# Spacing the loads of the first two heads and the start of the gate within one stage of a gated attention kernel

## The chip, the cores and the metric

The kernel runs on one core of a Trainium2 chip. The metric is the device time of one execution in microseconds. The kernel before took 2851.99 us (median of three runs, 2851.46 to 2855.48).

## The reference

Two attention blocks read the same input `x` (2048 rows of 1024) and are mixed row by row with a gate. Block A is a linear attention, block B a softmax attention, both with 32 heads of width 32. All tensors are float32. The two blocks are condensed below.

```python
def reference(A_x, A_wqkv, A_wo, B_x, B_wqkv, B_wo, gate_w):
    x = A_x
    g = _sigmoid((x * gate_w).sum(-1, keepdims=True))
    a = _A_ref(x, A_wqkv, A_wo)
    b = _B_ref(x, B_wqkv, B_wo)
    return g * a + (1 - g) * b
...
    # A: phi(t) = (t + 1 or exp(t)) + 1e-6
        kv = jnp.einsum("bhsd,bhse->bhde", phi(k), v)
        o = (phi(q) @ kv) / (phi(q) . sum(phi(k)) + 1e-6)
    # B:
        p = _softmax(q @ k.T * Dh ** -0.5)
        o = p @ v
    # both: o, heads side by side, @ wo
```

## The kernel before

Each float32 operand of a projection is split into a high and a low part, and a product of two such operands takes three matmuls (high by high, high by low, low by high; lines 152, 155 and 157). A first phase computes q and k of block B and the first half of its v, and writes them to DRAM (`qk`, `v`), together with the split rows of x (`xs`). Then a stage that this document calls the stage of v computes the second half of v, one unit for each of the 16 blocks of 128 rows. A unit is 24 matmuls: eight slices `k` of the contraction, three matmuls each. The stage also prepares the first two heads of block B, and computes the gate.

Three buffers hold x for these units, half a unit each: two DMAs of 256 KB (high and low part) fill one. `load_half(m)` issues such a load. It is called after the slices k = 3 and k = 7, for the half three places ahead, whose buffer has just become free.

Into the same units are threaded:

- `first`, a queue of 14 loads for heads 0 and 1. For each head, in this order: the first 512 columns of q (three DMAs of 64 KB, each into 32 partitions), the first 512 columns of k (likewise), the other 1536 columns of q (three DMAs of 192 KB), three further blocks of k (three DMAs of 64 KB each), and v (one DMA of 256 KB in pieces of 128 bytes).
- `gates`, a generator. Its first step loads the gate's weights, broadcast to 128 partitions (512 KB, into `zrep`), and the first block of x by rows (512 KB). Each later step computes one block's dot product on DVE (line 495) and loads the next block; two buffers take turns. Seventeen steps finish it.
- the scores of head 0 for the row maxima: one matmul (line 1123) and one reduction on DVE (line 1128), which frees the score's PSUM bank. 76 of them must be done before the heads' main loop (lines 1297, 1300) begins.
- the store of each unit's v (256 KB), after ScalarE has copied it out of PSUM.

The program is written out in order by a planner at build time. It keeps a clock per engine, with fixed costs for instructions and fixed guesses for when a load will be there, and emits the next item of four streams (`lin` for the units, `max` for the maxima, `head`, `out`) whose start its clock allows. Up to six scores may be emitted ahead of their due time; the others fall due evenly from the sixth unit's end to the fifteenth's. All DMAs of this stage are issued by SP, in the program's order, and every engine runs its own instructions in program order.

After the stage follow the 32 heads, with the linear attention's units between their matmuls, and the output projection.

Of the kernel before, what the change touches and what calls it, by code (L numbers as in the profile page):

```python
# [47 lines left out]
def kernel(  # L48
# [26 lines left out]
    TPC = C // P  # L75
# [63 lines left out]
    def wpart(k, p):  # L139

        o = ((k % 2) * 2 + p) * C
        return w_t[k // 2][:, o:o + C]
# [86 lines left out]
    def ended(items, *also):  # L229

        if any(item.end is None for item in items):
            return None
        return max([0.0, *also] + [item.end for item in items])
# [24 lines left out]
    def take(short=False):  # L258

        idle = ring(short)  # L260
        times = {b: ended(readers[b], free[b]) for b in idle}
        b = min(idle, key=lambda b: (times[b] is None, times[b] or 0.0))
        need(readers[b])
        free[b] = ended(readers[b], free[b])
        readers[b].clear()
        held[b] = True
        return b
# [469 lines left out]
    def pump_w(now=False):  # L737

        while next_w and (now or coming_w and coming_w[0][1] <= T["pe"]):
            follow, k, mark, eng = next_w.popleft()  # L740
            if not coming_w:
                more_w(True)
            split_w(*follow, k, *coming_w.popleft(), eng)
            mark.end = w_ready[k]
            if k + LEAD_W < NK:
                later_w.append((*follow, k + LEAD_W))
            more_w(now)
        more_w(now)
# [88 lines left out]
    def load_mix():  # L837
        assert not mix_here and not stores
        a, c = mix_todo.popleft()
        for i in range(HK):  # L840
            dma(mix_hi[i], a_wo[(a * HK + i) * P:(a * HK + i + 1) * P, c * C:(c + 1) * C])
        mix_here.append((a, c, T["pe"] + 11.0))
# [83 lines left out]
    def linear():  # L926
        extra = iter(())
        gates = gate()
        first = deque()
# [6 lines left out]
        for n, (i, t) in enumerate(units):  # L936
            kind, c = chunks[i]
            follow = chunks[i + 1] if i + 1 < len(chunks) else None
            lag = 2 if kind == "v" else 0

            def renew(k):

                mark = Later(None, 0.0, 0.0, 0, None)
                w_left[k][:] = [mark]
                next_w.append((follow, k, mark, nc.vector if kind == "v" else nc.gpsimd))
                pump_w(kind == "v")

            yield bank_at
            b = take()
            ps = bank[b]  # L950
            T["pe"] = max(T["pe"], free[b])
            lin_kind[0] = kind
            if (kind, c, t) in (("q", 1, 2), ("q", 1, 8), ("o", 0, 2), ("o", 0, 8)):
                load_mix()
            for k in range(NK):
                yield lambda: ended(w_left[k], w_ready[k], xp_ready.get(2 * n + k // HK, 0.0))
                need(w_left[k])
                stat = [xstat_lin(n, k, p) for p in range(2)]
                for m, _ in enumerate(three(ps, stat, (wpart(k, 0), wpart(k, 1)), k)):
                    lin_pe(1.0)  # L960
                    if m < 2:
                        yield always
                store_mix()
                if kind == "v":
                    if k % 2 and first:
                        first.popleft()()
                    if t >= 2 and (k == 2 or k == 6 and t % 2):
                        next(gates, None)
                if k % HK == HK - 1:
                    load_half(2 * n + k // HK + 3)  # L970
                if k == 0 and n + 7 == len(units) and not o_main[0]:
                    load_o(0)
                if k == 1 and n + 1 == len(units):
                    assert finished[0] >= H - 2
                    need(pr_left[extra_pr[2]])
                    xo_t[0] = big_tile(PR[extra_pr[2]], F32R)
                    split_o(0, slice(0, NK - 1))
                if k == NK // 2 and n + 1 == len(units) and over["head"]:
                    split_o(1, slice(0, NK - 1))
                if k == NK - 1:  # L980
                    yield from extra
                if follow and follow[0] == "o":
                    if t == NT - 1:
                        w_left[k].clear()
                        yield lambda: 0.0 if mixed.count((k // HK, follow[1])) == 8 * HK else None
                        load_wa(follow[1], k)
                    continue
                if follow and t == NT - 2 and k == 0:
                    yield lambda: None if mix_here or stores else 0.0
                if follow and t == NT - 2 and k < min(LEAD_W, NK):  # L990
                    coming_w.append(load_w(*follow, k, LEAD_W + 1))
                if follow and t == NT - 1 and k >= lag:
                    renew(k - lag)
            extra = iter(())
            e, r = mid[3 + n % 3], mid[6]
            if kind == "v":
                give(b, use("act", 0.5, T["pe"] + LATENCY["pe"]))
                v_out(c, t, ps, mid[11 - n % 2])
            elif kind == "kv":
                va = mid[7][:, (n % 2) * HC:(n % 2 + 1) * HC]  # L1000
                yield from keys_alone(n - 2)
                nc.scalar.copy(va, ps[:, HC:])
                use("act", 0.28, T["pe"] + LATENCY["pe"])
                end = phi(ps, e, HC)

                def more(end, c=c, t=t, e=e, ps=ps):
                    pk = e[:, :HC]
                    nc.vector.scalar_tensor_tensor(pk, pk, 1.0, ps[:, :HC], op0=ALU.min, op1=ALU.add)
                    z_end[c % 2] = use("pool", 0.69, end)
                    if t == 0:  # L1010
                        nc.gpsimd.tensor_copy(zsum[c % 2], pk)
                    else:
                        nc.gpsimd.tensor_add(zsum[c % 2], zsum[c % 2], pk)

                todo = [defer(more, end, 0.34)]
                give(b, 0.0, todo)
                keys(n, c, t, e, va, todo)
                if t == NT - 1:
                    extra = keysum(c)
            elif kind == "q":  # L1020
                yield lambda: None if n - 3 not in turned and chunks[units[n - 3][0]][0] == "q" else 0.0
                end = phi(ps, e, C)
                d = dn[n % 2]

                def sums(_, e=e, ps=ps):
                    nc.vector.scalar_tensor_tensor(ps, e, 1.0, ps, op0=ALU.min, op1=ALU.add)

                def scaled(_, c=c, ps=ps, r=r):
                    nc.vector.tensor_mul(r, ps, zrep[:, c * C:(c + 1) * C])

                last = []

                def dens(end, r=r, d=d, last=last):
                    nc.vector.tensor_reduce(d, r.rearrange("p (h d) -> p h d", d=DH), AX.X, ALU.add)
                    nc.scalar.add(d, d, eps)
                    last[0].at = use("act", 0.2, end)

                def divide(_, t=t, e=e, ps=ps, d=d):
                    nc.vector.reciprocal(d, d)
                    nc.vector.scalar_tensor_tensor(  # L1040
                        e.rearrange("p (h d) -> p h d", d=DH), ps.rearrange("p (h d) -> p h d", d=DH),
                        g_sb[:, t:t + 1], d.unsqueeze(2).to_broadcast([P, C // DH, DH]),
                        op0=ALU.mult, op1=ALU.mult)

                todo = chain(((sums, 0.63), (scaled, 0.63), (dens, 0.63), (divide, 0.9)), end)
                last.append(todo[-1])
                give(b, 0.0, todo)
                tasks.append((lambda todo=todo: None if kv_todo else both(ended(todo + o_left), o_free[(len(turned) + 1) % 2], bank_at()),
                              lambda n=n, c=c, t=t, e=e, todo=todo: queries(n, c, t, e, todo)))
            else:  # L1050
                res = mid[(7, 10)[n % 2]]
                give(b, use("act", 0.5, T["pe"] + LATENCY["pe"]))
                nc.scalar.copy(res, ps)
                dma(ra_d[t][:, c * C:(c + 1) * C], res)
            if follow and follow[0] != "o" and t == NT - 1:
                for k in range(NK - lag, NK):
                    renew(k)
# [661 lines left out]
```

## Time and profile before

| | |
|---|---|
| median of three runs | 2851.99 us |
| the profiled execution | 2853.72 us |
| its span, first to last instruction | 2852.0 us |
| mean granted clock of TensorE | 0.996 |
| DMA, mean over the span | 150 GB/s |

The page gives each engine's busy time, then the span in 40 slices of 71.3 us, of which each digit is a tenth of the slice. The slices of PE, its granted clock and DMA are the ones to look at here:

```profile
PE   9999998999999999999999999999999999999999
...
PEclk9999998999999999999999999999999999999999
DMA  8867679533344334333434344455656464534642
GB/s 276 248 222 234 208 217 286 169 96 104 96 126 104 102 99 123 96 101 97 132 97 107 97 130 133 147 172 172 195 180 184 132 165 137 157 109 133 198 150 78
```

The seventh slice (428 to 499 us) lies in the stage of v. It is the only one in which PE is under 90% busy and the granted clock under 0.9, and the one with the most DMA traffic.

In the views of single instructions a row gives the start in us from the span's beginning, the duration, the engine, the line, the operation with what it writes and reads, and in brackets how long the engine sat idle before it and what released it. SPq rows are the issuing of DMAs by SP: their duration is the time that SP spent on issuing, not the transfer's.

### The profile page before, as it was taken

The numbers are of one execution on the slowest core, as the hardware profiler recorded it, in microseconds if no ns is written. First come the engines' busy times: TensorE is split into PE (matmuls) and PEld (weight loads), VectorE is DVE, ScalarE is ACT, GpSimd is POOL, SyncE is SP. The second block draws the span as 40 slices with busy tenths as digits, with TensorE's granted clock in tenths as the row PEclk, the third lists the DMA queues.
The fourth block names the chain that finished last, engine by engine and source line by source line (L and its number), as shares of the span: only waits on it lengthen the run. The fifth ranks groups of instructions, "written<-read, shape, count | busy, mean of one in ns | idle before, by whom it ended". The sixth has DMA issues, their size and how long they took to land.

```text
span 2852.0 us, 46554 instructions
## 1 busy us (share of the span) xinstructions
PE 2823.2 (99%) x15944; PEld 2055.9 (72%) x15944; DVE 2232.2 (78%) x3659; ACT 1597.9 (56%) x2994; POOL 1910.0 (67%) x894
## 2 busy tenths in 40 slices
PE   9999998999999999999999999999999999999999
PEld 8888876677767776677667767777776766676787
DVE  7777755788888888888888888788878888887522
ACT  5334320466666666666666666566666666666400
POOL 0000010399999999999999999899889888885000
PEclk9999998999999999999999999999999999999999
DMA  8867679533344334333434344455656464534642
GB/s 276 248 222 234 208 217 286 169 96 104 96 126 104 102 99 123 96 101 97 132 97 107 97 130 133 147 172 172 195 180 184 132 165 137 157 109 133 198 150 78
DMA packets 376714, 428.56 MB, mean 150 GB/s; under 512 B 105007, under 2 KB 210735, under 8 KB 376477
## 3 DMA queue, kind: packets, MB, share of 16 engines
q1 hardware_dynamic: 362876, 412.47, 47.4%
q0 software_dynamic: 13600, 13.11, 3.4%
q8 instruction: 127, 2.08, 0.3%
q14 instruction: 111, 0.90, 0.1%
HBM read 298.06 MB, written 112.98 MB: 144 GB/s over the span
## 4 chain that ended last, share of the span: by engine, by line
PE 96%; DMA 2%; SPq 0%; issue 0%; ACT 0%; DVE 0%; POOL 0%; ACTq 0%
PE bank L1297 17%; PE bank L1123 16%; PE bank L152 15%; PE bank L1454 15%; PE bank L155 15%; PE bank L157 15%; DMA big<-xs 1%; PE bank L1188 1%; PE bank L906 1%; PE bank L795 0%; DMA v<-mid 0%; SPq L169 0%; DMA big<-qk 0%; PE bank L1180 0%; DMA big<-wa 0%
## 5 line engine op out<-in xcount | busy, mean ns | idle before, releaser
L1389 POOL TENSOR_TENSOR big<-big,big 128x512 f32<-128x512 f32 (+2 forms) x694 | 1644.8, 2374 | 116.3 <-ACT big L1300 73.6
L1128 DVE TENSOR_REDUCE mx<-bank 128x1 f32<-128x512 f32 x2048 | 1305.4, 683 | 269.4 <-PE bank L1123 265.5
L1300 ACT ACTIVATE big<-bank 128x512 f32<-128x512 f32 x2048 | 1180.4, 602 | 429.5 <-PE bank L1297 360.6
L1297 PE MATMUL bank<-big,big 128*128 128x512 f32 x1888 | 742.4, 394 | 0.6 <-ACT mid L355 0.5
L1123 PE MATMUL bank<-big,big 128*128 128x512 f32 x1888 | 738.5, 392 | 2.4 <-ACT big L1300 2.4
L152 PE MATMUL bank<-big,big 128*128 128x512 f32 x1600 | 627.5, 392 | 18.3 <-DMA big<-xs 18.2
L155 PE MATMUL bank<-big,big 128*128 128x512 f32 x1600 | 626.0, 391 | 0.0
L157 PE MATMUL bank<-big,big 128*128 128x512 f32 x1596 | 624.2, 391 | 0.4 <-DMA big<-xs 0.4
L1454 PE MATMUL bank<-big,mid 128*32 128x512 f32 x4096 | 454.1, 593 | 0.0
L1297 PEld LDWEIGHTS bank<-big,big 128*128 128x128 f32 x1888 | 354.0, 188 | 126.9 <-issue 46.9
L1123 PEld LDWEIGHTS bank<-big,big 128*128 128x128 f32 x1888 | 354.4, 188 | 77.6 <-ACT big L1300 5.4
L152 PEld LDWEIGHTS bank<-big,big 128*128 128x128 f32 x1600 | 301.8, 189 | 85.7 <-DMA big<-xs 17.5
L157 PEld LDWEIGHTS bank<-big,big 128*128 128x128 f32 x1596 | 300.9, 189 | 65.5 <-DMA big<-xs 2.6
L155 PEld LDWEIGHTS bank<-big,big 128*128 128x128 f32 x1600 | 302.0, 189 | 63.0 <-DVE big L294 0.4
L1454 PEld LDWEIGHTS bank<-big,mid 128*32 128x32 f32 x4096 | 142.3, 110 | 265.5 <-issue 265.5
L1080 POOL MEMSET big<- 32x512 f32 (+1 forms) x4 | 3.8, 952 | 385.8 <-PE bank L157 385.8
L1405 DVE TENSOR_TENSOR bank<-bank,big 128x512 f32<-128x512 f32 x364 | 251.7, 691 | 5.4 <-ACT big L1300 3.6
L152 PE MATMUL bank<-big,xh 128*128 128x512 f32 x384 | 150.6, 392 | 0.5 <-DMA xh<-xs 0.5
L155 PE MATMUL bank<-big,xh 128*128 128x512 f32 x384 | 150.2, 391 | 0.5 <-DMA big<-wa 0.5
L157 PE MATMUL bank<-big,xh 128*128 128x512 f32 x384 | 150.1, 391 | 0.1
L1385 POOL TENSOR_TENSOR big<-big,big 128x1536 f32<-128x1536 f32 (+1 forms) x31 | 122.6, 3955 | 35.9 <-ACT big L1300 32.7
L1463 ACT COPY mid<-bank 128x512 f32<-128x512 f32 x32 | 18.8, 588 | 207.5 <-PE bank L1454 207.5
(125 smaller groups left out, 1979.8 us busy)
## 6 DMA issues: line engine op xcount, KB each, us to landing
big<-xs SPq DMA_DIRECT2D x300, 256.0 KB
big<-qk SPq DMA_DIRECT2D x720, 64.0 KB
xh<-xs SPq DMA_DIRECT2D x148, 256.0 KB
qk<-mid SPq DMA_DIRECT2D x128, 256.0 KB
big<-oA SPq DMA_DIRECT2D x84, 256.0 KB
xs<-big SPq DMA_DIRECT2D x64, 256.0 KB
oA<-mid SPq DMA_DIRECT2D x64, 256.0 KB
big<-big POOLq DMA_DIRECT2D x50, 256.0 KB, 5.6
```

The costliest lines, as they stand in the source:

```text
L152: yield nc.tensor.matmul(ps, sh, mh_, start=(kt == 0), stop=False)
L155: yield nc.tensor.matmul(ps, sh, ml_, start=False, stop=(late and last))
L157: yield nc.tensor.matmul(ps, sl, mh_, start=False, stop=last)
L906: nc.tensor.transpose(pt[:, i * P:(i + 1) * P], pq[:, i * P:(i + 1) * P], ident)
L1123: nc.tensor.matmul(bank[b], q[:, t % TPC * P:(t % TPC + 1) * P], k[:, j * C:(j + 1) * C], start=True, stop=True)
L1128: nc.vector.tensor_reduce(m[:, t, j:j + 1], bank[b], AX.X, ALU.max)
L1297: nc.tensor.matmul(bank[b], k[:, t * P:(t + 1) * P], q_cols(h, j), start=True, stop=True)
L1300: nc.scalar.activation(pr_t[i][:, j * C:(j + 1) * C], bank[b], AF.Exp, scale=SCALE)
L1385: nc.gpsimd.tensor_add(lacc[:, :qp], pr(0)[:, :qp], pr(1)[:, :qp])
L1389: nc.gpsimd.tensor_add(lacc[:, sl], lacc[:, sl], pr(t)[:, sl])
L1405: nc.vector.tensor_add(lacc[:, qp:] if t == NT - 1 else l_b[:, :n], l_b[:, :n], src)
L1454: nc.tensor.matmul(av_b[j * DH:(j + 1) * DH, :], v[:, t, :], pr(t)[:, j * C:(j + 1) * C], start=(t == 0), stop=(t == NT - 1))
```

## The change

Two conditions inside a unit of v change. `first` hands out its loads at k = 1 in every unit and at k = 5 in every unit but the first, where it handed out one at each odd k. The gate takes a step at k = 3 and k = 7 of every unit from unit 5 on (`TPC` is 4), where it took one at k = 2 of every unit from unit 2 on and at k = 6 of the odd ones.

```diff
                 store_mix()
                 if kind == "v":
-                    if k % 2 and first:
+                    if first and (k == 1 or k == 5 and t):
                         first.popleft()()
-                    if t >= 2 and (k == 2 or k == 6 and t % 2):
+                    if t > TPC and k in (3, 7):
                         next(gates, None)
                 if k % HK == HK - 1:
                     load_half(2 * n + k // HK + 3)
```

The loads and the gate's steps stay the same in number, kind and order among themselves. Since the planner's clock sees other times for the loads of k and q, it also places the scores of head 0 elsewhere: the seven that stood in units 1 and 2 now stand among the others, from unit 6 on.

## The prediction

> **What bounds the kernel now.** I read the page first, then the waits of the stage of v, then that stage instruction by instruction on PE, SP and DVE.
>
> ```profile
> span 2852.0 us, 46554 instructions
> PE 2823.2 (99%) x15944; PEld 2055.9 (72%) x15944; DVE 2232.2 (78%) x3659; ACT 1597.9 (56%) x2994; POOL 1910.0 (67%) x894
> L1297 PE MATMUL bank<-big,big 128*128 128x512 f32 x1855 | 729.4, 395 | 0.1
> L1123 PE MATMUL bank<-big,big 128*128 128x512 f32 x1778 | 696.3, 392 | 1.0 <-ACT big L1300 1.0
> ...
> 397.00:531.00 134.00, 114.30 (x467) 90.15 (x466) 74.29 (x123) 13.84 (x25) 2.33 (x2) 0.92 0.84 262
> PE bank L152 <- DMA big<-xs: 18.2, 5, 8.9
> ```
>
> TensorE is the bound: 2823.2 of 2852.0 us. The two L lines are from the window behind 560 us: its largest PE groups waited 0.1 and 1.0 us in 2,290. The window 397 to 531 (busy PE, PEld, DVE, ACT, POOL, then granted clock, DMA share, GB/s) is the stage of v. There PE is busy 114.3 of 134 us at a clock of 0.92, DMA at 0.84. Five waits for x (xs) make 18.2 us. The change lives in this stage.
>
> I call the 12 matmuls that read one x buffer a half, and count the halves of the stage 0 to 31. Unit t has halves 2t and 2t+1, and the load of a half is issued three halves ahead.
>
> ```profile
> 402.52 0.39 PE L152 MATMUL bank<-big,xh 128*128 128x512 f32 x1
> ...
> 405.01 0.39 PE L157 MATMUL bank<-big,xh 128*128 128x512 f32 x1
> 407.21 0.68 PE L152 MATMUL bank<-big,big 128*128 128x512 f32 x1 [1.81 <-DMA big<-xs]
> 407.69 0.63 PE L155 MATMUL bank<-big,big 128*128 128x512 f32 x1
> ...
> 410.79 0.40 PE L157 MATMUL bank<-big,big 128*128 128x512 f32 x1
> ...
> 416.67 0.50 PE L152 MATMUL bank<-big,xh 128*128 128x512 f32 x1 [0.48 <-DMA xh<-xs]
> 422.46 0.47 PE L152 MATMUL bank<-big,big 128*128 128x512 f32 x1 [2.36 <-DMA big<-xs]
> 434.49 0.80 PE L152 MATMUL bank<-big,big 128*128 128x512 f32 x1 [8.86 <-DMA big<-xs]
> ...
> 438.32 0.39 PE L152 MATMUL bank<-big,big 128*128 128x512 f32 x1
> 445.27 0.79 PE L152 MATMUL bank<-big,big 128*128 128x512 f32 x1 [3.35 <-DMA big<-xs]
> 446.88 0.80 PE L157 MATMUL bank<-big,big 128*128 128x512 f32 x1 [0.40 <-DMA big<-xs]
> ...
> 451.98 0.40 PE L157 MATMUL bank<-big,big 128*128 128x512 f32 x1
> ```
>
> From 402.52 to 405.01 are eleven pitches of 0.226 us, so a half is 2.72 us. Between 405.01 and 451.98 start 94 matmuls (84 of halves 3 to 9, seven scores, three at the edges): 21.2 us at that pitch, in 46.97. So 25.7 us are lost here. Waits are 1.81 + 0.48 + 2.36 + 8.86 + 3.35 + 0.40 = 17.3. After three of them the pitch is 0.43: nine pitches take 3.58 us (407.21 to 410.79) and 3.83 (434.49 to 438.32) in place of 2.03, and from 445.27 the same goes on to 451.7. That costs 1.5 + 1.8 + 2.9 = 6.2. The remaining 2.2 are small gaps around half 5.
>
> **What the change removes, adds and moves.** No instruction is added or removed. On PE the two programs' orders differ from the first score on for about 830 matmuls and are identical behind that, so everything after the stage keeps its work and its bound; the sum is over the stage alone. Moved are the 14 parts of q, k and v of heads 0 and 1 (30 DMAs of 64 KB, 6 of 192, 2 of 256), from units 0 to 3 to units 0 to 7; the gate, from units 2 to 13 to units 5 to 13; and seven early scores, which ran in units 1 and 2 and now stand among the 76 that start in unit 6 (same work, no price).
>
> ```profile
> 401.10 2.73 SPq L169 DMA_DIRECT2D big<-qk  x6
> 403.92 0.84 SPq L169 DMA_DIRECT2D big<-xs  x2
> ...
> 418.47 0.81 SPq L169 DMA_DIRECT2D big<-xs  x2
> 419.38 0.38 SPq L169 DMA_DIRECT2D v<-mid  x1
> 419.81 1.40 SPq L169 DMA_DIRECT2D big<-qk  x3
> 421.26 0.46 SPq L169 DMA_DIRECT2D zrep<-in_gate_w  x1
> 421.77 0.42 SPq L169 DMA_DIRECT2D big<-in_x  x1
> 422.34 2.26 SPq L169 DMA_DIRECT2D big<-qk  x3
> 424.70 0.96 SPq L169 DMA_DIRECT2D big<-xs  x2
> 425.71 8.40 SPq L169 DMA_DIRECT2D big<-qk  x6
> ...
> 438.07 0.57 SPq L169 DMA_DIRECT2D mid<-v  x1
> 438.74 4.05 SPq L169 DMA_DIRECT2D big<-xs  x2
> 442.88 0.38 SPq L169 DMA_DIRECT2D big<-in_x  x1
> ...
> 425.00:430.00 5.00, 0.63 (x3) 0.19 (x1) 0.00 (x0) 0.00 (x0) 0.00 (x0) 0.78 1.04 244
> 430.00:435.00 5.00, 0.51 (x1) 0.50 (x2) 1.23 (x2) 0.00 (x0) 0.00 (x0) 0.50 0.85 186
> 455.00:460.00 5.00, 5.00 (x24) 4.14 (x23) 1.23 (x2) 0.59 (x1) 0.00 (x0) 1.00 1.01 376
> ```
>
> SP issues everything in program order, so what stands before an x load delays it. Prices, each for what is left after the change:
>
> Half 3 is issued at 403.92 behind six parts that took 2.73 us. Now three stand there, so it comes 1.37 earlier and 0.44 of the 1.81 is left. Ends 0.4 and 1.8; I take 0.6, and no slow pitch (the 0.48 wait at 416.67 had none).
>
> Halves 4 to 9: SP issues 11 DMAs a unit at 0.46, 5.1 us of the unit's 5.44, so it no longer falls behind. On the DMA engines x and v (1.25 MB) take 3.5 us at 376 GB/s and two small parts (0.38 MB) 1.6 to 2.1 at the 186 to 244 that the windows show while such parts run: 5.1 to 5.6 of 5.44, with 1.7 more where a long q part comes. Ends 0 and 5.0 (0.48, 2.36 and the gaps of before); I take 1.5.
>
> Half 10 now stands behind head 0's part of v. In the row at 438.74 the x loads behind such a part hold SP 4.05 us where 0.8 is usual. SP is then free some 2.2 us after half 7 and the load arrives 2.95 later (442.3 to 445.27), 5.2 of the 5.44 it has; its second part came 1.6 later still. Ends 0 and 3.35; I take 1.0.
>
> Half 13 is the large one. The gate's weights, its first x tile and the three long q loads of head 1 are issued together before half 13's load, as they were before half 7's (421.26 to 424.70). In the trace half 6 arrives at 422.46 and half 7 at 434.49: 12.0 us for v, three k parts, these five and x. The new order has the same list without the three k parts (192 KB at 244 GB/s, 0.8): 11.2 us behind half 12's arrival. PE has half 12 and five scores, 17 x 0.226 = 3.8 us, to fill it. So 7.4 us of wait, if half 12 arrives just as it is needed; ends 5.3 (half 12 two us early) and 8.9 (the row). Slow pitch behind it as at 434.49: 1.8, ends 1.5 and 2.9.
>
> Half 17 stands behind head 1's part of v and two gate tiles, as half 9 did, which waited 3.75. Scores make each half 3.6 us (31.5 matmuls a unit), so its two halves of lead hold 1.8 us more: 1.95, and half a chance of 2.9 of slow pitch, 1.4. Together 3.3; ends 0 and 6.6.
>
> ```profile
> 466.20 1.22 DVE L495 SCALAR_TENSOR_TENSOR big<-big,zrep 128x1024 f32<-128x1024 f32 x1
> 467.34 2.48 DVE L1128 TENSOR_REDUCE mx<-bank 128x1 f32<-128x512 f32 x4
> ...
> 431.08 1.23 DVE L495 SCALAR_TENSOR_TENSOR big<-big,zrep 128x1024 f32<-128x1024 f32 x1 [13.42 <-DMA big<-in_x]
> 448.20 1.23 DVE L495 SCALAR_TENSOR_TENSOR big<-big,zrep 128x1024 f32<-128x1024 f32 x1 [4.24 <-DMA big<-in_x]
> 527.10 0.50 PE L152 MATMUL bank<-big,big 128*128 128x512 f32 x1 [1.83 <-DMA big<-xs]
> ```
>
> Gate on DVE: it now comes every half from unit 5 on, where it came three times in two units. A half brings 3.75 reductions at 0.62 and 1.14 of gate, 3.47 us of DVE in 3.56 of PE; before it was 12.7 in 14.2 over two units. A gate step that waits for its tile holds up the reductions behind it, they hold the banks, and PE's next score waits for a bank; about five banks cover it. Ends 0 and 4; I take 0.9.
>
> The 1.83 at 527.10 stays: the loads of the maxima rows change places with one x load, under the same kv weights. Zero, between a gain and a loss of 1.8.
>
> Left: 0.6 + 1.5 + 1.0 + 7.4 + 1.8 + 3.3 + 0.9 = 16.5. Gone: 25.7 - 16.5 = 9.2 us. The profiled execution took 2853.72 (span 2852.0 and 1.7 around it) and becomes 2844.5; the median of the runs, 2851.99, becomes 2842.8.
>
> On the slow pitch the rows show a wait of 1.81 us followed by 0.43 and one of 2.36 followed by 0.23. [...]
>
> **Rivals.** A: the pile at the gate's start nearly vanishes. What speaks for it: its 2.16 MB at 376 GB/s would take 5.7 us, and the 12.0 were spent with six more parts queued behind. Half 13 then waits 1.9 with no slow pitch and half 17 2.0: left 0.6 + 1.5 + 1.0 + 1.9 + 2.0 + 0.9 = 7.9, time 2834. Against it: half 7's load was issued ahead of those six.
>
> B: the loss is only moved. Parts into 32 partitions take as long wherever they stand (244 and 186 GB/s at a full DMA share, against 376), and DMA is then behind in units 3 to 7. Half 10 waits 3.35, half 13 8.86 with 2.9 of slow pitch, half 17 3.75 with 2.9, halves 4 to 9 2.5, and 0.6 and 0.9 stay: 25.8, time 2852. Against it: later halves are longer by the scores. [...]
>
> C, slower: DVE becomes the bound. Two gate tiles are in turn, so a gate step can come every (load time + 1.2) / 2. From 442.88 to 448.20 a tile took 5.3 us: 3.25, under the 3.56 of a half. From 421.77 to 431.08 it took 9.3: 5.25, and 14 steps beside scores would lose 1.7 each, 24, less the banks' 4. With 9.2 gained elsewhere that is 2863. It decides from 7.8 us a tile on. Against it: once the parts are over, the full window 455 to 460 moves 376 GB/s.
>
> **How the numbers follow.** Forecast 0.62, A 0.14, B 0.16, C 0.08. The time is the forecast's, 2842.8, its own range 2839 to 2847 by the ends above. For 8 in 10 the range goes on towards A and B: 2836 to 2850. A measurement of this kernel can tell about 0.2%, 5.7 us, from no change. Faster by more: most of the forecast (0.55) and A, 0.69. Within: the rest of the forecast and B, 0.23. Slower: C, 0.08.
>
> **What would show it.** Right: PE's 18.2 us of waits for x shrink to about 12, the longest one 6 to 9 us at half 13, just after the load of the gate's weights; no slow pitch in the first three units; L1128's count and all behind unit 15 unchanged, 9 us earlier. Wrong: no wait over 3 us (A); waits for x still near 18 (B); PE idle in L1123 before a bank that DVE frees, with L495 waiting for in_x time after time (C).

## The result and the profile after

The changed kernel takes 2843.09 us (median of seven runs, 2841.04 to 2846.87) where the kernel before takes 2853.19 on the same chip (seven runs): a ratio of 0.9967, 95% interval 0.9955 to 0.9979. Timed a second time against another set of runs it was 2842.82 to 2852.38, ratio 0.9969 (0.9958 to 0.9979). So it is faster by 0.3%, some 10 us.

The page of the profiled execution (2843.68 us), with the granted clock and the traffic by slices of 71 us:

```profile
PEclk9999999999999999999999999999999999999999
...
GB/s 274 252 221 231 215 217 309 156 100 100 97 131 108 98 93 127 94 103 102 127 98 107 95 129 138 149 175 170 196 185 178 133 162 141 153 114 128 203 147 78
```

The 8 in the seventh slice of the granted clock is gone, and the same slice moves 309 GB/s instead of 286. The stage by itself, in the window of 397 to 531 us (columns as before) and in the waits of PE within it (total, times, longest):

```profile
397.00:531.00 134.00, 121.65 (x493) 92.13 (x492) 75.90 (x130) 17.98 (x33) 3.35 (x3) 0.97 0.88 277
```

```profile
PE bank L152 <- DMA big<-xs: 4.4, 5, 2.2
PE bank L157 <- DMA big<-xs: 2.1, 3, 1.4
PE bank L157 <- DMA xh<-xs: 1.7, 2, 1.3
PE bank L152 <- DMA xh<-xs: 1.4, 2, 1.1
```

PE fits 493 matmuls into the 134 us instead of 467, at a clock of 0.97 instead of 0.92. The waits for x (tiles `big` and `xh`) sum to 9.6 us, where the same window before had 19.1 (18.2 in the row that the prediction shows, and 0.5 and 0.4 in two smaller ones). The longest is 2.2, where it was 8.9. PE's single waits, with the slow stretches that belong to them:

```profile
403.01 0.39 PE L152 MATMUL bank<-big,xh 128*128 128x512 f32 x1
...
406.38 0.50 PE L152 MATMUL bank<-big,big 128*128 128x512 f32 x1 [0.48 <-DMA big<-xs]
...
408.54 0.50 PE L157 MATMUL bank<-big,big 128*128 128x512 f32 x1 [1.43 <-DMA big<-xs]
...
409.67 0.63 PE L152 MATMUL bank<-big,big 128*128 128x512 f32 x1
...
412.66 0.47 PE L155 MATMUL bank<-big,big 128*128 128x512 f32 x1
412.97 0.40 PE L157 MATMUL bank<-big,big 128*128 128x512 f32 x1
...
444.78 0.50 PE L152 MATMUL bank<-big,big 128*128 128x512 f32 x1 [2.25 <-DMA big<-xs]
...
445.75 0.50 PE L157 MATMUL bank<-big,big 128*128 128x512 f32 x1 [0.24 <-DMA big<-xs]
...
462.44 0.50 PE L152 MATMUL bank<-big,xh 128*128 128x512 f32 x1 [1.15 <-DMA xh<-xs]
...
464.47 0.79 PE L157 MATMUL bank<-big,xh 128*128 128x512 f32 x1 [1.29 <-DMA xh<-xs]
...
467.19 0.51 PE L152 MATMUL bank<-big,xh 128*128 128x512 f32 x1
467.55 0.39 PE L155 MATMUL bank<-big,xh 128*128 128x512 f32 x1
...
502.02 0.39 PE L1123 MATMUL bank<-big,big 128*128 128x512 f32 x1
```

The row at 444.78 is half 13, those at 462.44 and 464.47 are half 17, those at 406.38 and 408.54 half 3. The half 3 and half 17 waits are each followed by matmuls 0.43 us apart (409.67 to 412.66, and 464.47 to 467.19); the longer wait of half 13 is not.

To compare kernels, one number is used from here on. Half 2 starts at 403.01, and the last score ahead of half 27 at 502.02. In every order of this study 363 matmuls lie between these two points (25 halves of 12 and 63 scores), 82.26 us at the full pitch of 0.2266. What the stretch takes beyond that is called the loss: 99.01 - 82.26 = 16.75 us here (16.7 from here on), and in the kernel before, where the two points are 402.52 and 510.50, 107.98 - 82.26 = 25.7. That is 9.0 us gained inside the stage.

### The profile page after: what moved, and what is told of

Its sections match the earlier page's. It is cut to its first block, busy times and chain, and to the rows that moved or that the text cites. A ratio compares the mean times of both kernels' runs of the same rounds, so it can differ in the third digit from the quotient of the medians.

```text
span 2841.9 us, 46542 instructions
## 1 busy us (share of the span) xinstructions
PE 2823.3 (99%) x15944; PEld 2053.7 (72%) x15944; DVE 2229.5 (78%) x3659; ACT 1596.6 (56%) x2994; POOL 1909.1 (67%) x894
## 4 chain that ended last, share of the span: by engine, by line
PE 97%; DMA 2%; SPq 0%; ACT 0%; DVE 0%; issue 0%; ACTq 0%; DVEq 0%
PE bank L1297 17%; PE bank L1123 16%; PE bank L1454 16%; PE bank L152 15%; PE bank L155 15%; PE bank L157 15%; PE bank L1188 1%; DMA big<-xs 1%; PE bank L906 1%; PE bank L795 0%; DMA v<-mid 0%; DMA big<-qk 0%; DMA xh<-xs 0%; PE bank L1180 0%; DMA big<-in_x 0%; DMA big<-wa 0%
## 5 line engine op out<-in xcount | busy, mean ns | idle before, releaser
L1463 ACT COPY mid<-bank 128x512 f32<-128x512 f32 x32 | 18.8, 588 | 207.2 <-PE bank L1454 200.4
```

## The experiments

Ratios are to the kernel before, run on the same chip. The loss is that of the one profiled execution.

| kernel | median us (runs) | ratio, 95% interval | loss us |
|---|---|---|---|
| before; once more | 2853.19 (7); 2851.29 (1) | 1 | 25.7; 24.8 |
| changed | 2843.09 (7) | 0.9967, 0.9955 to 0.9979 | 16.7 |
| changed, once more | 2838.96 (1) | | 12.0 |
| changed, timed again | 2842.82 (8) | 0.9969, 0.9958 to 0.9979 | 11.8 |
| spacing of the loads alone | 2843.83 (8) | 0.9974, 0.9964 to 0.9985 | 16.0 |
| later gate alone | 2846.18 (11) | 0.9976, 0.9968 to 0.9985 | 18.8 |
| before, gate weights early | 2848.87 (11) | 0.9986, 0.9977 to 0.9995 | 20.1 |
| changed, first part later | 2840.60 (5) | 0.9962, 0.9950 to 0.9975 | 11.6 |
| changed, v parts later | 2840.39 (5) | 0.9962, 0.9949 to 0.9974 | 8.5 |
| changed, gate weights early | 2838.76 (5) | 0.9949, 0.9936 to 0.9961 | 10.2 |
| first part later, weights early | 2840.93 (5) | 0.9961, 0.9947 to 0.9974 | 12.7 |
| those two, v parts later, gate spread | 2838.46 (5) | 0.9947, 0.9933 to 0.9960 | 11.1 |
| those two, v parts later | 2837.34 (5) | 0.9945, 0.9933 to 0.9958 | 8.0 |

### Which half of the change does it

Two theories stood against each other for the 8.86 us wait of before. The crowd (C): two parts of q and k in every half keep SP and the DMA queues behind, so what helps is the wider spacing. The pile (P): the gate's weights, its first tile and long q parts come together ahead of one load of x, wherever the rest stands. Each half of the change was run alone.

Spacing alone, the gate where it was:

```diff
-                    if t > TPC and k in (3, 7):
+                    if t >= 2 and (k == 2 or k == 6 and t % 2):
```

> The loads of the two heads are spaced as in the changed kernel, the gate runs as before (from the third unit). Theory P, the pile: what cost half 7 its 8.9 us of wait and 1.8 of slow pitch is the burst of gate weights, first x tile and long q parts in front of one x load, so the half behind the gate's first step (6 or 7) still waits 6 us or more and the time is 2846 to 2850. Theory C, the crowd: what cost it is the number of parts in units 0 to 3, which kept SP and the DMA engines behind; then the half behind the gate's first step loses 3 us or less, as half 13 of the changed kernel did, and the time is 2840 to 2845. Before 2853.2, changed 2843.1.

The gate alone, four parts a unit as before:

```diff
-                    if first and (k == 1 or k == 5 and t):
+                    if k % 2 and first:
```

> The loads of the two heads stand as before, four parts a unit, the gate begins in the sixth unit as in the changed kernel. Theory P: halves 3 to 9 lose 12 us or less instead of 25.7, because the burst is no longer in front of half 7, and half 13 loses under 2 since no long q part is near; the time is 2838 to 2842. Theory C: halves 3 to 9 still lose 16 us or more and the time is 2846 to 2850. Seven early scores stand in units 1 and 2 again as before; that has no price in either theory.

PE's waits at halves 7 and 10 with the spacing alone, then at half 7 with the later gate alone:

```profile
421.63 0.50 PE L152 MATMUL bank<-big,big 128*128 128x512 f32 x1 [2.81 <-DMA big<-xs]
...
435.57 0.80 PE L157 MATMUL bank<-big,big 128*128 128x512 f32 x1 [1.80 <-DMA big<-xs]
```

```profile
428.89 0.66 PE L152 MATMUL bank<-big,big 128*128 128x512 f32 x1 [2.43 <-DMA big<-xs]
```

SP ahead of half 7 with the spacing alone:

```profile
408.43 1.66 SPq L169 DMA_DIRECT2D big<-qk  x3
410.19 0.84 SPq L169 DMA_DIRECT2D big<-xs  x2
...
413.88 0.35 SPq L169 DMA_DIRECT2D zrep<-in_gate_w  x1
414.90 0.35 SPq L169 DMA_DIRECT2D big<-in_x  x1
415.50 1.38 SPq L169 DMA_DIRECT2D big<-xs  x2
```

With the spacing alone, half 7 (421.63) waits 2.81 instead of 8.86, and loses 3.6, near what the crowd had. But the run does not take away the crowd alone. The weights and the first tile still stand ahead of half 7's load (415.50), while the long q parts (408.43) now go ahead of half 6's (410.19), so the pile is no longer whole. The most is lost at half 10 here (435.57), 5.9 us with slow pitch. With the later gate alone half 7 (428.89) waits 2.43, and halves 3 to 9 still lose 16.5 of the 18.8 us, as the crowd had it. The later gate saves 25.7 - 18.8 = 6.9 us, and the two gains (9.7 and 6.9) do not add up to that of both (9.0 in the first profile of the changed kernel, 13.7 and 13.9 in two later ones): the 8.86 needed at least two things at once, the weights and either the crowd or the long q parts right behind them, and each half of the change breaks it. Which of the two it is these runs do not tell. By the times, neither spacing alone (0.9974) nor the later gate alone (0.9976) can be told from the whole change (0.9967 and 0.9969).

### What the long wait of before was made of

The kernel before was profiled once more, to see whether its waits come back, and then with one edit: the gate's weights (512 KB) are loaded right ahead of the stage, so they are not in the pile.

> The kernel before, profiled once more. If the 8.9 us of wait at half 7 belong to its order of loads, this trace shows 7 us or more there again and 23 to 28 us lost in halves 3 to 9 (25.7 in the first trace). If they were a chance of that one execution, the wait is under 5 us and the loss under 21.

```diff
     def gate():
-        dma(zrep, bass.AP(tensor=gate_w.tensor, offset=gate_w.offset, ap=[[0, P], [1, D]]))
...
     quads(1, lambda: load_v1(raw_a, range(KH)), spill_rest(1))
+    dma(zrep, bass.AP(tensor=gate_w.tensor, offset=gate_w.offset, ap=[[0, P], [1, D]]))
```

> The kernel before, with the gate's weights loaded ahead of the stage; PE's order is that of the kernel before. Theory: in the kernel before the weights stand in a queue that is already behind, and the 3.7 us between the landings of the third k part and of the weights' last engine fall on PE in full, with one spell of slow pitch: half 7 waits 4 to 6 instead of 8.9, time 2846 to 2849. Rival: the crowd of parts alone makes half 7 late; the wait stays at 7 or more, time 2850 to 2853.

PE at half 7 in the repeat, and in the kernel with early weights (there with SP's issue of that load, and what follows it):

```profile
435.70 0.80 PE L152 MATMUL bank<-big,big 128*128 128x512 f32 x1 [6.82 <-DMA big<-xs]
```

```profile
429.89 0.50 PE L152 MATMUL bank<-big,big 128*128 128x512 f32 x1 [2.15 <-DMA big<-xs]
```

```profile
424.37 0.81 SPq L169 DMA_DIRECT2D big<-xs  x2
425.23 4.56 SPq L169 DMA_DIRECT2D big<-qk  x6
```

The repeat waits 6.82, a little under the expected 7, and loses 24.8. Without the weights the wait is 2.15, less than was expected; half 7 starts 5.5 us after its load's issue (424.37 to 429.89) instead of 9.8 (424.70 to 434.49), and the six parts behind it take SP 4.56 us instead of 8.40. The other waits of before remain and its time is 2848.87. So the weights are a main part of the 8.86 but not of the 25.7.

The traces also record when the 16 shares of each transfer report their end. In both profiles of the kernel before, the shares of the weights end far apart, over 3.5 us (424.81 to 428.30) and 3.1 us, and all that stands behind them, up to half 7's x, stays as far apart. In the three profiles of the changed kernel the weights' shares end within 0.8 to 1.3 us of each other, with the spacing alone within 1.0. Half 7's x has its first share at 431.42 and its last at 434.45, and PE starts at 434.49. In the changed kernel the shares of half 13's x end within 1.0 us, so by estimate some 2 us of the long wait are this spread. SP's 8.40 us is a result of it and not a cause: the second of the six parts is issued at 428.31, just behind the weights' last share. Why the shares fell apart stays open.

### How the changed kernel varies

The changed kernel was profiled again, twice, because the stretches of slow pitch in its first profile stood behind short waits.

> The changed kernel once more, one profile. Theory: the waits belong to the order of loads and come again at half 13 (2 to 3 us), half 17 (1 to 1.5 in one place) and half 3 (0.3 to 2); only the stretches of slow pitch behind the short waits (3.1 us of loss at half 3, 4.4 at half 17 the first time) may or may not come again, so the loss up to half 17 lies between 12 and 17. Rival: the 3.1 and 4.4 belong to the order of loads too, and both come again within 0.5.

> The changed kernel once more, timed. Theory: the order of loads sets waits that come every time (about 12 us of loss up to half 17), and stretches of slow pitch behind the short ones that come in some executions only (up to 5 us more); the single executions then spread over 2839 to 2847, their median is 2841 to 2844, and the ratio to before 0.9958 to 0.9970. The profile shows half 13 waiting 2 to 3 us, and at half 3 and half 17 either 1 to 1.9 or 3 to 4.4 of loss, nothing between. Rival: the 16.7 of the first profile are what the order costs, the 12.0 of the second were an outlier; the loss is 16 to 17 again.

PE's largest waits in the one (2838.96 us) and in the other (2841.30):

```profile
442.65 0.80 PE L152 MATMUL bank<-big,big 128*128 128x512 f32 x1 [2.22 <-DMA big<-xs]
...
502.07 0.28 PE L1140 MATMUL bank<-ident,mneg 128*16 128x128 f32 x1 [1.28 <-DVE mneg L1134]
```

```profile
443.80 0.50 PE L152 MATMUL bank<-big,big 128*128 128x512 f32 x1 [2.66 <-DMA big<-xs]
...
445.00 0.50 PE L157 MATMUL bank<-big,big 128*128 128x512 f32 x1 [0.46 <-DMA big<-xs]
...
503.99 0.28 PE L1140 MATMUL bank<-ident,mneg 128*16 128x128 f32 x1 [1.80 <-DVE mneg L1134]
```

The loss is 12.0 and 11.8, at the lower end of the theory and far from the rival's 16.7. Half 13 waits 2.2 to 3.1 us in all three profiles. Half 3 loses 4.1, 1.8 and 1.8 us, half 17 4.4, 1.3 and 0.5 in the order of the three profiles (the 0.5 lies under the theory's lower figure of 1). Slow pitch stood behind half 3 and half 17 the first time, and behind half 13 the other two times. So up to 4.9 us of the loss differ between executions of one and the same kernel, about as much as many edits of this stage are worth. The eight runs of the second timing, 2841.30 to 2847.50, fit that.

At L1140 PE transposes the row maxima of head 0 and must have DVE's last one. That wait was 0.47 in the kernel before. It is 1.28 and 1.80 us here, where PE is earlier, and the first profile shows none.

### Each remaining wait by its suspected transfer

The first part of q one half later (half 3's load no longer stands behind it):

```diff
-                    if first and (k == 1 or k == 5 and t):
+                    if first and (k == 5 or k == 1 and t):
```

> The changed kernel, but the first q part of head 0 goes at k = 5 of unit 0, behind half 3's load instead of in front of it; nothing else moves and PE's order is the same. Theory: half 3 of the changed kernel loses 3.1 us (0.5 and 1.4 of wait, the rest slow pitch) because three q DMAs stand in front of it; it then loses under 0.7 and keeps the full pitch, and the time is 2840 to 2841. Rival: half 3's second DMA is late because the DMA engines are out of step after the stores of q and k; moving three small loads gives 1.3 us at most, a slow spell may stay, time 2842 to 2843.

The two parts of v in units 10 and 12 instead of 3 and 7:

```diff
-            first.append(lambda h=h: load_v(h))
+            first.append(lambda: None)
...
+                    if k == 1 and t in (10, 12):
+                        load_v(t // 12)
```

> The changed kernel, but the two v parts (pieces of 128 bytes) go in units 10 and 12 instead of 3 and 7; nothing else moves and PE's order is the same. Theory: the v part holds SP and so the x loads behind it, which is what halves 10 and 11 (2.2 us) and half 17 with its slow spell (4.4) lose; both losses go, nothing comes back in units 10 and 12 because the gate's pace and the scores leave room there, time 2837 to 2839. Rival: half 17 loses because two gate tiles a unit put DMA behind from unit 5 on; then half 17 still loses 3 or more and the time is 2841 to 2843.

The gate's weights ahead of the stage, by the same edit as above, now in the changed kernel:

> The changed kernel, with the gate's weights loaded ahead of the stage, during the last products of q and k; PE's order is the same. Theory: the weights cost only the 1.3 us between the landings of the third long q part and of the weights in the queue; half 13's wait of 2.5 falls to about 1.2, time 2840 to 2842.5. Rival: the broadcast read puts the DMA engines out of step for some us more (as the 12.0 us of the kernel before suggested); then half 13 no longer waits and half 17 loses under 2 as well, time 2837 to 2839.5.

PE with the first part later; with the parts of v later; with the weights early:

```profile
406.37 0.50 PE L157 MATMUL bank<-big,big 128*128 128x512 f32 x1 [0.26 <-DMA big<-xs]
```

```profile
442.11 0.50 PE L152 MATMUL bank<-big,big 128*128 128x512 f32 x1 [2.18 <-DMA big<-xs]
...
443.08 0.50 PE L157 MATMUL bank<-big,big 128*128 128x512 f32 x1 [0.24 <-DMA big<-xs]
...
501.16 0.28 PE L1142 MATMUL bank<-ident,mneg 128*16 128x128 f32 x1 [2.27 <-DVE mneg L1136]
```

```profile
442.19 0.50 PE L152 MATMUL bank<-big,big 128*128 128x512 f32 x1 [1.04 <-DMA big<-xs]
...
443.51 0.50 PE L157 MATMUL bank<-big,big 128*128 128x512 f32 x1 [0.58 <-DMA big<-xs]
```

With v later PE waits once, 0.36 us at half 27 (495.15), between 443.08 and the transpose of the maxima (two lines further down in that kernel, L1142): half 17's wait is gone. In the two kernels below that move v, half 17 loses nothing either, and the six profiles with the changed gate that leave v in unit 7 lose 0.5 to 4.4 us there, so this cause is shown. What is gained there is partly given back in the transpose's 2.27 us for DVE, and the time, 2840.39, lies between the theory's and the rival's. Half 13 waits 1.04 + 0.58 with early weights, where the three profiles of the changed kernel have 2.2 to 3.1. The first x tile and the three q parts still stand ahead of it, and taking those out was not tried. The time with early weights, 2838.76, is the rival's; the wait of 1.6 is nearer to the theory's 1.2 than to none.

For the first part the picture is weaker than this one profile suggests. Half 3 lost 0.6, and in the three kernels below that also move the part 0.0, 0.4 and 2.1, against 1.8 to 4.1 in the changed kernel. The expected 2840 to 2841 came out, but the changed kernel by itself also reached 2838.96 in one execution.

### Together

All three edits, with the parts of v in units 9 and 11 and the gate spread over more units:

```diff
+                    if k == 1 and t in (9, 11):
+                        load_v(t // 11)
-                    if t > TPC and k in (3, 7):
+                    if t > 2 and (k == 3 or k == 7 and t % 2):
```

> The changed kernel with all that the first runs point to: the first part behind half 3's load, the v parts in units 9 and 11, the gate's weights ahead of the stage, and three gate steps in two units from the fourth unit on instead of four from the sixth. If the losses are those of the queue, half by half: half 3 loses under 1, halves 4 to 12 about 3, halves 13 to 17 under 2, and DVE, with a gate step less in two units, no longer makes the maxima's transpose wait (2.3 us in the run with the v parts late); time 2832 to 2836. Rival: DMA is at its limit over units 0 to 7 whatever the order; then what half 13 and 17 no longer lose comes up in halves 9 to 12, time 2838 to 2841.

The first part later and the weights early, nothing else:

> The changed kernel with the first part at k = 5 of unit 0 and the gate's weights loaded before the stage. Theory (each loss has its own transfer): half 3 loses 0.6 as with the later part alone, half 13 1.5 to 2.2 as with the early weights alone, half 17 1.3 to 1.9; the stage loses 7 to 9 in all, and the time is 2837 to 2839. Rival (what one place gives up another takes): 10 or more is lost, and the time is no better than with one of the two alone, 2839 to 2841.

All three edits, with the gate as the change has it:

> The changed kernel with the first part at k = 5 of unit 0, the weights before the stage and the two parts of v in units 9 and 11; the gate where the change put it, not spread from unit 3. Theory: half 3 loses under 0.6, halves 10 and 11 about 1.5, half 13 1 to 2, half 17 0 to 0.5, and the maxima's transpose waits 1 to 2.5 us for DVE, since PE is ahead of it: 6 to 8 lost, time 2836 to 2838. Rival: DVE's backlog or DMA takes back what is gained; 9 to 11 lost, 2838 to 2840.

PE where the gate is spread, then with the gate as in the change:

```profile
436.23 0.65 PE L152 MATMUL bank<-big,xh 128*128 128x512 f32 x1 [3.08 <-DMA xh<-xs]
```

```profile
407.67 0.50 PE L157 MATMUL bank<-big,big 128*128 128x512 f32 x1 [1.73 <-DMA big<-xs]
```

Spreading the gate brings its tiles among the parts of q and k, and a wait of 3.08 us returns at half 11: what one place gives up another takes, as the rival said. Left where the change put it, the stage loses 8.0 us, half 17 nothing, and the time is 2837.34, as the theory said but for half 3's 1.73. Without the later parts of v the loss is 12.7 (half 17 takes 3.9 of it, with slow pitch) and the time 2840.93, the rival's. The best version is thus 5.5 us below the changed kernel's 2842.82; against the kernel before, its interval overlaps one of the changed kernel's and touches the other (0.9955 and 0.9958), so the two are not told apart with certainty.

## Why the prediction came out

The predicted 2842.8 us was met by both medians, 2843.09 and 2842.82. The sum behind it was met less well. Its terms, and the loss of the three profiles of the changed kernel at the same places (each half with the wait ahead of it, slow pitch with the wait that it follows):

| place | forecast us | first | second | third |
|---|---|---|---|---|
| half 3 | 0.6 | 4.1 | 1.8 | 1.8 |
| halves 4 to 9 | 1.5 | 1.9 | 1.9 | 1.4 |
| half 10 | 1.0 | 1.2 | 1.2 | 0.8 |
| half 11 | 0 | 1.1 | 1.6 | 1.6 |
| half 13, with slow pitch | 7.4 + 1.8 | 3.1 | 4.2 | 5.3 |
| half 17 | 3.3 | 4.4 | 1.3 | 0.5 |
| banks and other | 0.9 | 0.9 | 0.0 | 0.4 |
| sum | 16.5 | 16.7 | 12.0 | 11.8 |

**Half 13 is the step that failed.** It was priced as "the same list without the three k parts", 11.2 us behind half 12's arrival, which made a loss of 9.2 us with its slow pitch; it lost 3.1 to 5.3. The rows of SP in the changed kernel, and of PE at half 12:

```profile
435.09 1.81 SPq L169 DMA_DIRECT2D big<-qk  x3
436.94 0.42 SPq L169 DMA_DIRECT2D zrep<-in_gate_w  x1
437.41 0.42 SPq L169 DMA_DIRECT2D big<-in_x  x1
437.94 0.86 SPq L169 DMA_DIRECT2D big<-xs  x2
438.96 2.14 SPq L169 DMA_DIRECT2D big<-qk  x3
```

```profile
438.52 0.39 PE L152 MATMUL bank<-big,big 128*128 128x512 f32 x1
```

Half 12 starts at 438.52 without a wait; the last share of its high part came at 437.39, 1.1 us early, which is within what the sum allowed. From there to half 13's start at 444.78 are 7.4 us where the sum had 11.2; from the load's issue at 437.94 they are 6.8, where before it was 9.8. So the price of the list was wrong: the 12.0 us of the kernel before were more than its transfers need. By the estimate above some 2 us of them are the spread of the shares. The queues were about as far behind both times: the low part of the last x load ahead of the list took 4.1 us from its issue to its last share before (418.92 to 423.02) and 4.0 now (434.19 to 438.19).

Two things do differ: six parts followed the load before and three now, and the long q parts stood behind the weights before (422.34) and stand ahead of them now (435.09). With six followers and no weights the load took 5.5, so the followers alone are not it. No run changes that order alone, so what else shortened the list stays open. By the prediction's own signs, the one that it gave for rival A came out, no wait over 3 us in one piece, and not its own 6 to 9. The waits for x came to 9.6 us where it had about 12, and slow pitch did come in the second unit, in one profile of three (409.67). Rival A gave half 13 a wait of 1.9 (measured 2.2 to 3.1) and had a chance of 0.14. Its 2834 failed on the other terms.

**Half 3 was sized too low, and half 11 had no price.** At half 3 the forecast of the wait, 0.44, was right to 0.04 for the high part of x (0.48 at 406.38). The low part, the load's second DMA, cost another wait of 1.43 that was not in the sum, nor was the slow pitch behind the two. Half 10 came out as forecast, and with the part of v moved it loses nothing. But half 11 loses 1.1 to 1.6, and 1.4 with v moved, so that is not from the part of v. Why a low part follows its high part as late as it does stays open.

**Halves 4 to 9 and half 17 were right,** the first within 0.4, the second in cause and within its ends of 0 and 6.6. That a slow stretch follows was given half a chance, and it followed in one of three profiles, behind waits of 1.15 and 1.29 us (462.44, 464.47).

**Banks and DVE.** No wait for a bank appeared. The gate's step on DVE that waits longest for its tile, behind the first, in the changed kernel:

```profile
466.19 1.23 DVE L495 SCALAR_TENSOR_TENSOR big<-big,zrep 128x1024 f32<-128x1024 f32 x1 [1.60 <-DMA big<-in_x]
```

DVE waits up to 1.6 us for a tile, as rival C had it, but the banks cover that. At the end of the maxima PE then waits 1.28 and 1.80 at L1140, which the prediction did not have.

**The sum against the median.** The three profiles lose 13.5 us on average in the stage and the two of before 25.3, a gain of 11.7. Behind half 26 the kernel before loses 3.7 us more up to the stage's end, in both its profiles, the changed one 3.9, 5.0 and 5.7: up to 2 us go back, most of them at L1140. The 1.83 of 527.10, which was to stay, shrank to 0.74, 1.26 and 0.81 in the three profiles; but the next half, which waited for nothing before, waits 0.9 to 1.6. So the median's 9.6 to 10.1 came with a larger gain in the stage than the 9.2 forecast, and a part returned behind it. That the time was met to 0.3 us is in good part luck: half 13 was priced some 5 us too high, halves 3 and 11 some 3.4 too low, and the wait at L1140 was not in the sum. The rivals B and C are out: B asked for a loss of 25.8, C for PE idle before banks.

## What to carry to other kernels

Price a wait for a load from its issue to its use, do not take the time that a list of transfers once took as the price of its bytes (here 12.0 us for the old list, and then 7.4 for nearly the same one), and give each DMA of the load a term of its own: here the second one cost a further wait of up to 1.8 us. A wait that two causes make together falls when either goes, so the gains of two edits do not add. Where the bound engine is freed, look at what it meets next (here DVE's last row maximum), and profile more than once before a single short wait is credited to an edit.

## What the hardware showed that was not expected

The slow pitch comes in stretches whose ends keep a fixed beat in both traces. In the changed kernel's rows above, slow pitch ends within 412.66 to 412.97 and within 467.19 to 467.55; each of these two matmuls was partly slow. The slow pitch is 0.427 (seven take 2.99 us from 409.67 to 412.66), the full one 0.227. Of the first one's pitch of 0.31, (0.31 - 0.227) / (1 - 0.227/0.427) = 0.18 us were slow, and of the second's 0.36 0.28, so the change falls at 412.84 and 467.47, 54.63 us apart. The starts of the last partly slow matmuls in two stretches of the kernel before:

```profile
438.07 0.41 PE L157 MATMUL bank<-big,big 128*128 128x512 f32 x1
...
451.75 0.39 PE L155 MATMUL bank<-big,big 128*128 128x512 f32 x1
```

With the first end at 410.79 in the prediction's rows, the ends come out in the same way at 410.81, 438.12 and 451.76, the later ones 27.31 and 40.95 us from the first. The profile's record of the granted clock has the same stretches within 0.04 us: the clock is 0.50 from 409.42 to 412.83 and from 464.03 to 467.44 in the changed kernel, from 407.36 to 410.78, from 427.84 to 438.08 and from 444.91 to 451.74 in the kernel before, and 1.00 everywhere else between 397 and 531. The shortest last 3.41 us, the longer ones 10.24 and 6.83, three and two times as much, and all three distances are whole multiples of 3.41 too: 16, 8 and 12. Such a point, a whole number of 3.41 us away from an end, is called an edge here.

In these two traces slow pitch goes with how much waiting lies between two edges, not with how long one wait is. In the changed kernel the 3.41 us from 406.0 to 409.4 had 0.37 + 1.43 = 1.8 us of waits and the next 3.41 were slow; the 2.25 of half 13 (442.53 to 444.78) straddles an edge at 443.56, 1.0 to one side and 1.2 + 0.24 to the other, and nothing was slow. In the kernel before, the 2.36 at 422.46 straddles 421.04 (3 x 3.41 behind 410.81) in the same way and no slow pitch followed, while the 1.81 at 407.21 lay between two edges, and it did. Of these four cases those with up to 1.5 us between two edges were not followed by slow pitch, and those with 1.8 were. Two other runs make the border less sharp. With the spacing alone the 2.81 at 421.63 puts 1.9 ahead of one edge, 420.72 (six times 3.41 ahead of that run's end of slow pitch at 441.18), and nothing was slow; with the first part later and the weights early 1.08 and 0.61 us (460.08, 461.43), 1.69 between two edges, were followed by slow pitch from 462.1 to 465.5. No run here was made to find the border. Behind a slow stretch less was enough once: 0.76 us (0.36 + 0.40 in 444.91 to 448.32 of the kernel before), and so its wait of 3.35 cost 6.83 us at half the clock. By estimate 3.41 us of it cost about 1.6 us (3.41 x (1 - 0.227/0.427)). The beat lies differently in each execution: in the third profile of the changed kernel slow pitch ends at 449.18, 10.7 times 3.41 behind the 412.84 of the first. There 1.45 us of half 13's 2.66 and its 0.46 lie between two edges (442.35 to 445.77), and slow pitch followed. In the second, half 13 waited 2.22 and its first matmul took 0.80 (442.65), where the first profile has 2.25 and 0.50 (444.78). So the same wait costs a slow stretch in one execution and not in the next, which fits the stretches moving from halves 3 and 17 to half 13 among the three profiles.
